# Matrix-LSTM attention before two mixtures of experts: decay by matmuls over gate rows, row-tiled scores, and a new order of attention, routing and experts

## Chip, cores and metric

One core of one Trainium2 chip. The metric is device time in microseconds (us) of one launch; lower is better.

## The reference, cut to what matters

```python
B, H, S, D = 2, 8, 768, 40                       # attention, token by token
m_new  = maximum(f_gate[t] + m, i_gate[t])
f_stab, i_stab = exp(f_gate[t] + m - m_new), exp(i_gate[t] - m_new)
C = f_stab * C + i_stab * outer(v[t], k[t])
n = f_stab * n + i_stab * k[t]
y[t] = sigmoid(o_gate[t]) * (C @ q[t]) / maximum(abs(n @ q[t]), 1)
x = y as (1536, 320)                             # tokens of both batches
noisy = x @ w_gate + log1p(exp(x @ w_noise)) * noise
top2 of 8 experts a token, weights softmax(top2)
out[token] += weight * (relu(x[token] @ w1[e]) @ w2[e])         # F = 1024
out2 = sum over 4 experts of p[:, e] * (relu(out @ v1[e]) @ v2[e])
```

## The kernel before, in words

**Attention.** The 768 tokens of a batch are cut into 6 chunks of 128, so 12 chunks run one behind the other, batch 0 first. The gates stand as 16 rows (batch and head) of 768 columns. `gates` (L234) forms running maxima and decay sums on DVE (VectorE) in four parts (chunk 0, chunk 1, chunks 2 and 3, chunks 4 and 5; each part holds both batches). `gates_turn` transposes the result to token rows, `gates_out` writes the decay sums LF and their exponentials to DRAM. For a chunk, `o_load` brings LF back, copied to all 128 partitions (tile A, 512 KB), and the state's decay gb; `o_decay` makes 8 exponentials of 128x128 on ACT (ScalarE, L333), one per head with that head's bias, and POOL (GpSimd) masks them (L335). `o_S` computes scores: kp holds 4 heads in partitions 0 to 39 and 4 in 64 to 103, zero elsewhere, and each of 8 matmuls contracts 104 rows (L342). `o_M` multiplies scores by A on DVE (L348), `o_AV` and `o_inter` sum values and the state's share (L407, L400), `o_U`, `o_Cu`, `o_Cg` carry the state C, `o_qg` scales queries by gb on POOL (L353), `o_tp` and `o_x` transpose and normalise into x (L428), `o_store` writes x to DRAM. `o_xp` transposes x for the router, `o_lp` and `o_lt` make its logits: three matmuls with the router weights stationary, a copy, a transpose and a reduction.

**The order.** `STEP` (L48) is one step of the pipeline, four pieces; a word such as S1+1 is an operation with the chunk it works on, counted from the step's. 16 steps make 64 pieces. Two strings weave them with other work: in `PLAN1` A is a piece, r a piece of the routing of batch 0, w a split of a weight into two fp32r parts, z and o single loads; `PLAN2` does the same for batch 1 beside the first expert units. The strings set the order in which the program is written and hence the priorities; a scheduler then places each engine's instructions. `route(b, h)` (L473) ranks the 8 logits of half of a batch, counts slots, and scatters token numbers to DRAM with one indirect DMA on POOL per chunk and choice (L540): 8 for the first half, 4 for the second. Then `xload` (L592) gathers an expert's tokens (xe, L598) and `prep` (L605) transposes and splits them.

**Experts.** `UNITS` lists 12 units: experts 0 to 3 on batch 0 (256 columns each), expert 3 on batch 1 (256, unit 4), experts 4 to 7 on both (448), experts 2, 1, 0 on batch 1. A unit is 64 matmuls of stage 1 (L194: 8 blocks of 128 hidden rows, 8 products each) and stage 2 (L208: 3 products per block and token tile). Units 0 to 3 are woven with `PLAN2`; unit 4 is loaded and prepared only after unit 3, when the attention's pools are closed. The second mixture (`moe2`) runs 4 experts over the 1536 tokens in groups of `G2` = 384 columns, 4 groups an expert; `combine` gathers the first mixture's rows into its input.

## Time and profile before

| | us |
|---|---|
| median of 3 runs | 706.52 (706.26, 713.24, 706.52) |
| profiled execution | 711.51, its span 709.5 |
| PE / DVE / ACT / POOL busy in the span | 683.9 / 370.2 / 265.6 / 128.4 |
| mean granted TensorE clock | 0.972 of full speed |

Rows of the profile were read from the one profiled execution. PE is TensorE's matmuls, "PEclk" the granted clock (1.00 is 2.4 GHz, 0.50 is 1.2 GHz). The span has three parts: attention and the first routing up to about 112 us, the 12 expert units up to about 344 us, the second mixture to the end.

### The profile page before, as it was taken

To read this page: it belongs to the slowest core of one execution; us is meant where nothing else is said; L and a number is where in the kernel's file an instruction comes from. 1 tells how busy PE (TensorE), PEld (TensorE's weight loads), DVE (VectorE), ACT (ScalarE), POOL (GpSimd) and SP (SyncE) were. 2 spreads that over 40 slices of the span, in tenths; PEclk is the share of its full clock that TensorE was granted. 3 is DMA by queue.
4 is the path that set the end of the run, shared out by engine and by line. 5 is a ranking of instruction groups with operands and counts; after the bars stand their busy time and mean duration, and the time that the engine had idled before them with its cause. 6 is when DMAs were issued, how large, how long until landed. Compare 5 with 4: busy or idle time off the path is not lost.

```text
span 709.5 us, 11969 instructions
## 1 busy us (share of the span) xinstructions
PE 683.9 (96%) x4683; PEld 656.0 (92%) x4683; DVE 370.2 (52%) x819; ACT 265.6 (37%) x533; POOL 128.4 (18%) x183
## 2 busy tenths in 40 slices
PE   8997888999899999999999999999999999999997
PEld 6776668999799999999999999999999999999997
DVE  7767778885466565658855325332252322423321
ACT  5557546752353444445532214221132212312210
POOL 5453782054501101124042000000000000000000
PEclk7897699999999999999999999999999999999999
DMA  6789657765556454467651004100041000000000
GB/s 186 218 247 283 189 167 237 219 190 146 149 185 192 123 150 139 141 198 232 198 181 52 1 1 120 45 1 1 1 130 34 1 1 16 23 1 29 28 29 31
DMA packets 39948, 80.07 MB, mean 113 GB/s; under 512 B 9376, under 2 KB 16464, under 8 KB 39888
## 3 DMA queue, kind: packets, MB, share of 16 engines
q1 hardware_dynamic: 36496, 70.39, 33.1%
q0 software_dynamic: 3392, 8.86, 4.4%
q8 instruction: 39, 0.64, 0.4%
q14 instruction: 21, 0.17, 0.1%
HBM read 70.20 MB, written 9.04 MB: 112 GB/s over the span
## 4 chain that ended last, share of the span: by engine, by line
PE 89%; DMA 4%; DVE 4%; issue 2%; POOL 0%; ACT 0%; another core or an unknown queue 0%; SPq 0%; ACTq 0%; DVEq 0%
PE z L194 25%; PE z L208 24%; PE s L194 15%; PE s L208 12%; PE sp L342 3%; PE hp L407 2%; PE s L204 1%; PE lp L449 1%; DMA raw<-w 1%; DMA kp<-kT 1%; PE lb L324 1%; PE pa L612 1%; PE hp L400 1%; PE tp L415 1%; DMA gb<-gd 1%
## 5 line engine op out<-in xcount | busy, mean ns | idle before, releaser
L211 ACT ACTIVATE hh<-z 128x384 fp32r<-128x384 f32 x128 | 62.4, 492 | 220.4 <-PE z L194 219.3
L194 PE MATMUL z<-x2h,w1hi 128*128 128x384 f32 x384 | 128.6, 335 | 0.0
L208 PE MATMUL z<-w2lo,hh 128*128 128x320 f32 x384 | 118.8, 309 | 0.5 <-issue 0.3
L208 PE MATMUL z<-w2hi,hh 128*128 128x320 f32 x384 | 119.0, 310 | 0.0
L208 PE MATMUL z<-w2hi,hl 128*128 128x320 f32 x384 | 118.7, 309 | 0.0
L212 DVE SCALAR_TENSOR_TENSOR hl<-z,hh 128x384 fp32r<-128x384 f32 x128 | 69.9, 555 | 84.2 <-ACT hh L211 84.1
L208 PE MATMUL s<-w2hi,hh 128*128 128x320 f32 x448 | 107.8, 313 | 1.2 <-DVE hh L212 1.1
L194 PE MATMUL z<-x2h,w1lo 128*128 128x384 f32 x384 | 107.8, 334 | 0.0
L194 PE MATMUL z<-x2l,w1hi 128*128 128x384 f32 x256 | 85.6, 334 | 0.0
L194 PE MATMUL s<-xh,w1hi 128*128 128x256 f32 (+1 forms) x288 | 84.6, 312 | 0.6 <-issue 0.6
L208 PEld LDWEIGHTS s<-w2hi,hh 128*128 128x128 f32 x448 | 76.8, 188 | 2.7 <-DVE hh L212 1.7
L175 DVE TENSOR_TENSOR w1lo<-raw,w1hi 128x768 fp32r<-128x768 f32 x60 | 57.3, 957 | 38.7 <-ACT w1hi L174 38.0
L175 DVE TENSOR_TENSOR w2lo<-raw,w2hi 128x640 fp32r<-128x640 f32 x60 | 49.2, 822 | 52.5 <-ACT w2hi L174 48.7
L208 PEld LDWEIGHTS z<-w2hi,hl 128*128 128x128 f32 x384 | 72.2, 188 | 0.5 <-issue 0.5
L208 PEld LDWEIGHTS z<-w2lo,hh 128*128 128x128 f32 x384 | 72.2, 188 | 0.4 <-issue 0.4
L208 PEld LDWEIGHTS z<-w2hi,hh 128*128 128x128 f32 x384 | 72.2, 188 | 0.0
L194 PEld LDWEIGHTS z<-x2h,w1hi 128*128 128x128 f32 x384 | 72.1, 188 | 0.0
L194 PE MATMUL s<-xh,w1lo 128*128 128x256 f32 (+1 forms) x288 | 70.6, 309 | 1.2 <-issue 1.2
L194 PEld LDWEIGHTS z<-x2h,w1lo 128*128 128x128 f32 x384 | 70.3, 188 | 0.0
L208 PE MATMUL s<-w2lo,hh 128*128 128x320 f32 x224 | 69.1, 309 | 0.0
L174 ACT CAST w2hi<-raw 128x640 fp32r<-128x640 f32 x60 | 43.4, 728 | 64.5 <-PE s L204 22.9
L174 ACT CAST w1hi<-raw 128x768 fp32r<-128x768 f32 x60 | 49.9, 836 | 45.0 <-PE s L194 18.3
(188 smaller groups left out, 1036.2 us busy)
## 6 DMA issues: line engine op xcount, KB each, us to landing
raw<-w SPq DMA_DIRECT2D x44, 384.0 KB
raw<-w SPq DMA_DIRECT2D x44, 320.0 KB
raw<-v SPq DMA_DIRECT2D x16, 384.0 KB
A<-LFd SPq DMA_DIRECT2D x10, 512.0 KB
raw<-v SPq DMA_DIRECT2D x16, 320.0 KB
kv<-kv SPq DMA_DIRECT2D x12, 324.0 KB
Yd<-ys SPq DMA_DIRECT2D x8, 320.0 KB
qt<-qT SPq DMA_DIRECT2D x12, 208.0 KB
```

The source lines that it names most:

```text
L174: nc.scalar.copy(hi, raw)
L175: nc.vector.tensor_sub(lo, raw, hi.bitcast(F32))
L194: nc.tensor.matmul(out_ps, l, r, start=(i == 0), stop=(i == len(seq) - 1))
L204: nc.tensor.matmul(yp, both[f], r[:, k], start=(f == 0 and i == 0), stop=(f == NF - 1 and i == 1))
L208: nc.tensor.matmul(yp, l, r, start=(f == 0 and i == 0), stop=(f == NF - 1 and i == 2))
L211: nc.scalar.activation(hh, src, AF.Relu)
L212: nc.vector.scalar_tensor_tensor(hl, src, 0.0, hh.bitcast(F32), ALU.max, ALU.subtract)
L324: nc.tensor.matmul(lp[:, j, :], rowsel[:, 4 * g + j, :], LF[:, i, :], start=True, stop=True)
L342: nc.tensor.matmul(sp[:, j, :], t["kp"][:, 4 * g + j, :], t["qt"][:, j, :], start=True, stop=True)
L400: nc.tensor.matmul(hp[:, p, :], Cs[c % 2][:, p, :], t["qg"][:, p, :], start=(p == 0), stop=False)
L407: nc.tensor.matmul(hp[64 * j : 64 * j + 41, p, :], t["kv"][:, 4 * j + p, D:], t["A"][:, 4 * j + p, :], start=False, stop=(p == 3))
L415: nc.tensor.transpose(tp[:, p, :], st[i]["hs"][:, p, :], ident[:105, :105])
```

## The change

Gate rows stand on all 128 partitions (8 copies of the 16, loaded as 768 KB), and `gates_terms` turns them into two operands tk and tq, so that a single matmul per 4 heads gives all the exponents of A in PSUM and a single exponential makes A (`o_decay`). gb comes by a matmul and an exponential too (`o_gb`). The loads of A and gb, and the transposes for the bias, are gone. The products tq and tk are 128x512 each; those of chunk 0 run on DVE, those of chunks 1 to 5 on POOL. Scores are 8 matmuls of 40 rows, alternating between two row groups and two PSUM banks; k comes in one load of 208 KB. The router's logits are 3 matmuls with x stationary and a copy. The scatters are letters s of the plans, one or two beside a piece; the second half's routing (q), the end of the routing (F), gathers (X) and the first `prep` (P) have letters as well. The first expert begins with 12 pieces left. The gathers and `prep` of unit 4 move into unit 3. `G2` is 512, and the first group's stage 1 runs ahead of `combine(1)`.

```diff
-G2 = 3 * P
+G2 = 4 * P
-LEAD = 6
-PLAN1 = "AAAAAAAAAAAzAAoAAAArrwArAwArrrrrArArrrrwrAAArrrArrArAwrrArArAArrrrArrrArA"
+PLAN1 = "Az A Al Al Ag Al Aw A Aw A Aw A Aw A A A Ar Ar Ar Ar Ar Ar Ass Asr Asq Asq Asq Asq Asq Aq Ass AssF Aq AX A AF AF A AP"
...
-    "U+0 D1+2 kw+1 M1+0 loadk+2 S0+1 lp-2 store-3",
-    "qg+1 tp-1 x-1 Cu-1 Cg+0 load+3 inter+0 M0+0 D0+3 lt-2",
-    "",
-    "S1+1 xp-1 AV+0",
+    "U+0 D0+2 D1+2 kw+1 M1+0 loadk+2 lg-2 store-2",
+    "tp-1 x-1 qg+1 M0+0 inter+0 load+3 Cg+0",
+    "G+2",
+    "xp-1 S+1 AV+0 Cu+0",
...
+    def gates_terms(part):
+        n = PARTS[part]
+        nc.scalar.copy(LFh[:, n], LF[:, n])
+        nc.scalar.copy(ash[:, n], asr[:, n])
+        nc.vector.tensor_scalar(flat(LF, n), flat(LF, n), low, keys, ALU.mult, ALU.add)
+        nc.vector.scalar_tensor_tensor(flat(LF, n), flat(LFh, n).bitcast(F32), qsel, flat(LF, n), ALU.mult, ALU.add)
...
+        eng = nc.vector if part == 0 else nc.gpsimd
+        for c in range(n.start, n.stop):
+            wide = lambda x: x.unsqueeze(1).to_broadcast([P, 4, P])
+            eng.tensor_mul(tq[:, c], wide(LF[:, c]), head.unsqueeze(2).to_broadcast([P, 4, P]))
+            last = eng.tensor_mul(tk[:, c], wide(asr[:, c]), quarter.unsqueeze(2).to_broadcast([P, 4, P]))
...
     def sigmoid(b):
+        nc.scalar.preload_act_table_set("sigmoid_and_others")
         nc.scalar.activation(xs[b], xs[b], AF.Sigmoid)
+        nc.scalar.preload_act_table_set("natural_log_exp_and_others")
...
-        for h in range(4 * g, 4 * g + 4):
-            src = t["lb", g][:, h - 4 * g, :] if ("lb", g) in t else A[:, h, :]
-            last = nc.scalar.activation(A[:, h, :], src, AF.Exp, bias=as_t[:, c, b * H + h : b * H + h + 1])
...
+        dp = psum([P, 4, P], "dp")
+        nc.tensor.matmul(dp, tk[:, c, 2 * b + g], tq[:, c], start=True, stop=True)
+        nc.scalar.activation(A, dp, AF.Exp)
...
-    def o_S(i, g):
+    def o_S(i):
         t = st[i]
-        sp = psum([P, 4, P], "sp")
+        sp = [psum([P, 4, P], "sp") for _ in range(2)]
         for j in range(4):
-            nc.tensor.matmul(sp[:, j, :], t["kp"][:, 4 * g + j, :], t["qt"][:, j, :], start=True, stop=True)
...
+            for g in range(2):
+                r = slice(64 * g, 64 * g + D)
+                nc.tensor.matmul(sp[g][:, j, :], t["kp"][r, j, :], t["qt"][r, j, :], start=True, stop=True)
...
-    for w in PLAN1:
...
-    xload(0)
-    xload(1)
-    drain_n(A, LEAD)
-    prep(0)
...
+    drain(follow(PLAN1, 0, 0))
+    RST = follow(PLAN2, 1, ALONE)
...
+    mj_cm = tc.tile_pool(name="m1j", bufs=2, side="right")
+    joint.append(mj_cm.__enter__())
+    xload(ALONE)
+    if ALONE not in preps:
+        prep(ALONE)
+    drain(moe1(ALONE))
...
+                if g == 0:
+                    next(c1)
+                    drain_n(unit, NF // 2)
```

What the new order makes of the engines' queues shows at three places. First PE (matmuls) in one step of the attention, from the state update up to the scores. Before:

```order
L376 MATMUL up_501<-kv,kw 40x41 x8
L342 MATMUL sp_520<-qt,kp_164 128x128 x4
L449 MATMUL lp_525<-xt,wgn 32x128 x3
L415 MATMUL tp_533<-ident,hs 128x105 x4
L400 MATMUL hp_559<-qg,C_188 105x128 x4
L460 MATMUL lt_571<-ident,ls 128x96
L342 MATMUL sp_574<-qt,kp_164 128x128 x4
L438 MATMUL xp_579<-ident,x_85 128x128 x2
L439 MATMUL xp_579<-ident,x_85 64x128
L407 MATMUL hp_559<-A,kv 41x128 x8
```

After, the same step (dp is the exponent of A, gp that of gb):

```order
L388 MATMUL up_604<-kv,kw 40x41 x8
L333 MATMUL dp_614<-tq,tk 128x512
L333 MATMUL dp_618<-tq,tk 128x512
L462 MATMUL lp_627<-wgn,xt_202 128x16 x3
L427 MATMUL tp_633<-ident,hs 128x105 x4
L412 MATMUL hp_649<-qg,C_199 105x128 x4
L342 MATMUL gp_666<-tq,over_91 104x512
L419 MATMUL hp_649<-A,kv 41x128 x8
L450 MATMUL xp_670<-ident,x_103 128x128 x2
L451 MATMUL xp_670<-ident,x_103 64x128
L354 MATMUL sp_676<-qt,kp 128x128
L354 MATMUL sp_677<-qt,kp 128x128
```

The two blocks of four scores have become one run that alternates between two banks (six more rows like the last two follow), three matmuls of 512 columns are new, and the transpose lt is gone.

Second POOL, from batch 0's first scatter (Td) to the experts' first gather (xe). Before:

```order
L540 DMA Td<-toki,slot_89 10240x1 x8
L335 AFFINE_SELECT A<-A 128x512
L368 TENSOR_TENSOR C_190<-C_188,gb 40x4x41 x2
L335 AFFINE_SELECT A<-A 128x512
L353 TENSOR_TENSOR qg<-qt,gb 104x512
L368 TENSOR_TENSOR C_188<-C_190,gb 40x4x41 x2
L335 AFFINE_SELECT A<-A 128x512
L540 DMA Td<-toki,slot_89 10240x1 x2
L335 AFFINE_SELECT A<-A 128x512
L540 DMA Td<-toki,slot_89 10240x1 x2
L353 TENSOR_TENSOR qg<-qt,gb 104x512
L368 TENSOR_TENSOR C_190<-C_188,gb 40x4x41 x2
```

After, up to the last scatter:

```order
L549 DMA Td<-toki,slot_107 10240x1 x2
L335 AFFINE_SELECT A<-A 128x512 x2
L549 DMA Td<-toki,slot_107 10240x1 x5
L365 TENSOR_TENSOR qg<-qt,gb 104x512
L380 TENSOR_TENSOR C_199<-C_197,gb 40x4x41 x2
L549 DMA Td<-toki,slot_107 10240x1
L335 AFFINE_SELECT A<-A 128x512 x2
L380 TENSOR_TENSOR C_197<-C_199,gb 40x4x41 x2
L365 TENSOR_TENSOR qg<-qt,gb 104x512
L549 DMA Td<-toki,slot_107 10240x1 x4
L335 AFFINE_SELECT A<-A 128x512 x2
L380 TENSOR_TENSOR C_199<-C_197,gb 40x4x41 x2
```

The lump of 8 scatters is cut into 2, 5 and 1 with the attention's masks and products between; before, two masks and a qg follow up to the gather, after, one qg. Between first scatter and first gather the list is the same: 12 scatters, 6 masks, 3 qg, 6 C.

Third PE where unit 4's tokens (pa, pb) are transposed. Before, behind the last stage-2 matmul of unit 3 and ahead of unit 4's first:

```order
L208 MATMUL s_141_2374<-w2hi,hh 128x320
L612 MATMUL pa_2441<-ident,xe 128x128 x2
L613 MATMUL pb_2442<-ident,xe 64x128
L612 MATMUL pa_2441<-ident,xe 128x128 x2
L613 MATMUL pb_2442<-ident,xe 64x128
L194 MATMUL s_144_2471<-xh,w1hi 128x256
```

After, between stage 1 and stage 2 of unit 3:

```order
L214 MATMUL s_157_2286<-xh,w1lo 128x256
L624 MATMUL pa_2311<-ident,xe 128x128 x2
L625 MATMUL pb_2312<-ident,xe 64x128
L624 MATMUL pa_2311<-ident,xe 128x128 x2
L625 MATMUL pb_2312<-ident,xe 64x128
L228 MATMUL s_160_2325<-w2hi,hh 128x320
```

The transposes now have the 48 stage-2 matmuls of unit 3 between them and unit 4. Behind the first expert's first matmul, the attention still has to issue on PE: before, xp, a rest of AV, lp, lt, tp, xp, lp, lt; after, tp, the state's share, xp, AV, lp, tp, xp, lp.

## Rows read from the trace of the kernel before

**Rows 1.** Page, part 1: engine, busy us (share of the span), instructions.

```profile
PE 683.9 (96%) x4683; PEld 656.0 (92%) x4683; DVE 370.2 (52%) x819; ACT 265.6 (37%) x533; POOL 128.4 (18%) x183
```

**Rows 2.** Chain that ended last: start us, us, what.

```profile
52.30 7.55 DMA kp<-kT
...
176.90 3.33 DMA xe<-Xall,tok
...
197.61 12.82 PE s L194 x64
...
401.48 11.10 PE z L194 x64
...
694.25 10.58 PE z L208 x72
```

**Rows 3.** Windows: stretch, length, each engine's busy us (instructions), clock, DMA share, GB/s.

```profile
core 0: us, PE busy (x) PEld busy (x) DVE busy (x) ACT busy (x) POOL busy (x), PEclk, DMA share, GB/s
27.80:111.20 83.40, 70.20 (x678) 56.55 (x676) 62.12 (x196) 48.26 (x124) 48.37 (x59) 0.86 0.76 223
41.80:47.70 5.90, 5.90 (x72) 5.00 (x71) 3.90 (x13) 3.45 (x12) 3.43 (x5) 1.00 0.88 272
53.70:65.70 12.00, 8.44 (x73) 6.80 (x73) 9.20 (x32) 9.24 (x18) 3.41 (x5) 0.72 0.98 269
65.70:75.40 9.70, 8.10 (x74) 6.29 (x73) 8.89 (x25) 7.18 (x20) 6.75 (x7) 0.82 0.95 277
75.40:88.00 12.60, 11.03 (x72) 8.36 (x73) 8.67 (x39) 5.92 (x13) 9.04 (x12) 0.52 0.57 166
...
112.40:130.60 18.20, 18.20 (x142) 16.87 (x141) 15.97 (x39) 13.35 (x24) 3.49 (x3) 1.00 0.77 229
...
161.70:176.50 14.80, 14.80 (x115) 14.76 (x114) 8.36 (x25) 4.24 (x8) 6.65 (x7) 1.00 0.54 160
...
176.50:180.60 4.10, 2.23 (x16) 1.46 (x15) 1.92 (x4) 0.85 (x2) 2.90 (x4) 1.00 0.72 213
...
180.60:197.40 16.80, 15.65 (x118) 15.19 (x119) 7.60 (x11) 6.40 (x12) 7.59 (x8) 1.00 0.48 142
```

**Rows 4.** POOL's timeline at scatters and gathers, and PE's first prep: start us, us.

```profile
70.46 1.21 POOL L540 DMA_INDIRECT Td<-toki,slot  x1 [1.56 <-DVE xt L442]
...
101.80 1.01 POOL L598 DMA_INDIRECT xe<-Xall,tok  x1 [0.15 <-issue]
...
109.77 0.38 PE L612 MATMUL pa<-ident,xe 128*128 128x128 f32 x2
```

**Rows 5.** Groups by form: line, engine, operation, count, busy us, mean ns.

```profile
L540 POOL DMA_INDIRECT Td<-toki,slot x24 | 26.9, 1119 | 35.0 <-DVE tmp L545 26.4 <-issue 5.7 <-DVE xt L442 1.6
L335 POOL TENSOR_SCALAR_AFFINE_SELECT A<-A 128x512 f32<-128x512 f32 x24 | 16.7, 701 | 30.9 <-ACT A L333 27.4 <-issue 2.6 <-DMA kv<-kv 0.5
L353 POOL TENSOR_TENSOR qg<-qt,gb 104x512 f32<-104x512 f32 x10 | 13.6, 1358 | 0.0
L368 POOL TENSOR_TENSOR C<-C,gb 40x164 f32<-40x164 f32 x16 | 8.5, 533 | 6.7 <-PE lt L460 1.7 <-DVE sl L527 1.7 <-DVE C L387 1.6
...
L348 DVE TENSOR_TENSOR A<-sp,A 128x512 f32<-128x512 f32 x20 | 13.8, 688 | 5.3 <-DMA qt<-qT 1.5 <-POOL A L335 1.5 <-issue 0.9
...
L272 ACT ACT_TABLE_LOAD x2 | 2.6, 1283 | 0.8 <-PEq L1039 0.8
```

**Rows 6.** PE's timeline in one step, at full clock: values, then half the scores.

```profile
49.37 1.07 PE L407 MATMUL hp<-A,kv 128*41 128x128 f32 x16
50.37 1.16 PE L342 MATMUL sp<-qt,kp 104*128 104x128 f32 x8
```

**Rows 7.** DVE's normalisation beside POOL's product, and the same one later, alone: timelines.

```profile
27.93 2.31 DVE L428 TENSOR_TENSOR x<-xo,rd 128x320 f32<-128x320 f32 x1
...
28.64 1.25 POOL L353 TENSOR_TENSOR qg<-qt,gb 104x512 f32<-104x512 f32 x1
...
65.75 0.48 DVE L428 TENSOR_TENSOR x<-xo,rd 128x320 f32<-128x320 f32 x1
```

More of the change, by code (lines that the diff above doesn't have):

```diff
@@ L548, in route, with scatter, routed_ @@
         yield
-        if h == 0:
-            return
+    scats = []
+    def scatter():
+        b, k, c = scats.pop(0)
+        s = nc.gpsimd.indirect_dma_start(out=Td, out_offset=bass.IndirectOffsetOnAxis(ap=slot[b][:, k, c : c + 1], axis=0), in_=toki[:, b * NC + c : b * NC + c + 1], in_offset=None)
+        for q in rt[b]["prev"]:
+            tc.declare_no_dep(s.ins, q.ins, reason="distinct rows")
+        rt[b]["prev"].append(s)
+    def routed_(b):
+        assert not scats
+        nl, selb, sel = (rt[b][n] for n in ("nl", "selb", "sel"))
+        routed.add(b)
         nc.sync.dma_start(tok[b].rearrange("p e j -> p (e j)"), Td[: P * E1 * NCOL].rearrange("(p j) o -> p (j o)", p=P))
@@ L589, in xload @@
     def xload(n):
[L590 removed]
+        if n >= len(UNITS) or n in xes or n in preps or not routed.issuperset(UNITS[n][1]) or (n > ALONE and not joint):
             return
@@ L906, in body @@
     m1 = m1_cm.__enter__()
-    nc.sync.dma_start(noise, d["noise"])
     def init():
         nc.sync.dma_start(Td[: P * E1 * NCOL].rearrange("(p j) o -> p (j o)", p=P), zidx)
-    def routes(b):
-        for h in range(2):
-            yield from route(b, h)
-        routed.add(b)
     def splits():
@@ L921, in splits, with follow @@
             yield
-    R0 = routes(0)
-    W0 = splits()
-    for w in PLAN1:
-        if w in "zo":
-            init() if w == "z" else og_load(1)
-        else:
-            next({"A": A, "r": R0, "w": W0}[w], None)
-    drain(W0)
-    drain(R0)
-    xload(0)
-    xload(1)
-    drain_n(A, LEAD)
-    prep(0)
-    def rest():
-        R1 = routes(1)
-        for w in PLAN2:
-            if w == " ":
-                yield
-            else:
-                next({"A": A, "r": R1}[w], None)
-        drain(A)
-        drain(R1)
-    RST = rest()
+    def follow(plan, b, first):
+        r, q, f, w = route(b, 0), route(b, 1), routed_(b), splits()
+        for group in plan.split():
+            for t in group:
+                if t in "Arqfw":
+                    next({"A": A, "r": r, "q": q, "w": w}[t], None)
+                elif t == "F":
+                    next(f, None)
+                elif t == "X":
+                    xload(first)
+                    xload(first + 1)
+                else:
+                    {"s": scatter, "l": w_load, "P": lambda: prep(first), "z": init, "g": lambda: sigmoid(1)}[t]()
+            yield
+        for g in (A, r, q, f):
+            assert next(g, None) is None or g is A
+    drain(follow(PLAN1, 0, 0))
+    RST = follow(PLAN2, 1, ALONE)
     for n in range(ALONE):
@@ L970, in body @@
     x2l = x2p.tile([P, 2, B * S], F32R, name="x2l")
-    for n in range(ALONE, LAST0 + 1):
+    for n in range(ALONE + 1, LAST0 + 1):
         drain(moe1(n))
```

264 lines of the change are left out of this document (111 added, 153 removed).

## Prediction, made before the changed kernel was run

> **What bounds the kernel now.** I read the page's busy times first: PE is busy 96% of the span [rows 1], so a gain must take work from PE or close the few holes in it. The chain of waits shows where these are. From 401 us on it alternates between 64 stage-1 and 72 stage-2 matmuls without a gap, up to 704.8 [rows 2]: that part is PE alone. The holes lie ahead of the experts, and at one unit border, where PE waits for gathered tokens [rows 2]. The windows measure the first part [rows 3]: from 27.8 to 111.2 us, ten steps of the attention, PE is busy for 70.2 of 83.4 us, at a granted clock of 0.86, and DVE for 62.1. One step takes 5.90 us when nothing disturbs it, and is then all PE; but 53.7 to 65.7 takes 12.0 (DMA share 0.98, and the chain waits 7.55 us for kp [rows 2]), 65.7 to 75.4 takes 9.7 with DVE busy for 8.89 of them, and 75.4 to 88.0 takes 12.6, at a clock of 0.52, beside the lump of eight scatters on POOL. What counts is when the first expert runs densely: 112.4 us in this trace. Behind that, all is a sum of PE work.
>
> The sum below is made against the profiled execution's 711.5 us, 5.0 above the median of 706.5. The 5.0 are subtracted at the end.
>
> **The change, part by part.**
>
> *Second mixture, 512 instead of 384 columns.* A stage-1 matmul of 384 columns takes 11.10/64 = 173.4 ns, one of 448 12.82/64 = 200.3 [rows 2]: 0.42 ns a column, so 227 ns for 512 and 14.53 us for 64. 16 groups of 11.10 are 177.6, 12 of 14.53 are 174.3: **-3.3**. Stage 2 has the same matmuls. The combination of batch 1 must now be done during the first group; its gathers lie beside 14.5 us of stage 1. If they came late, a gather's wait like 3.33 us [rows 2] would take all of this back.
>
> *Unit 4.* Between unit 3 and unit 4, 4.10 us pass with PE busy for 2.23, some of that thinly [rows 3]. The transposes, about 1 us, stay; moved behind stage 1 of unit 3 they have the 48 stage-2 matmuls ahead of unit 4 as cover for the splits on ACT and DVE: -3.1. Unit 4 itself took 16.80 us, unit 3 14.80 and without a hole [rows 3]; I take back 1.5 of the 2.0, since the gathers of unit 5 still come after the pools close. Together **-4.6**, bounds 0 (the gather is late in its new place too) and -6.1 (the whole 4.10 and the whole 2.0).
>
> *What is left of the attention behind the first expert's start.* Before, the stretch 112.4 to 130.6 took 18.2 against 14.8 of unit 3 [rows 3]: 3.4 us of attention. After, PE still issues tp, the state's share, xp, AV, lp and again tp, xp, lp. An undisturbed step of 5.90 [rows 3] without its scores (twice 1.16 [rows 6]) is 3.6; tp, xp and lp a second time add about half of that, 1.9: 5.5. **+2.1**, bounds 0 (they fall into holes) and +4.
>
> *The start of the experts.* Two sums, for DVE and for POOL, since both wait and are waited for.
>
> DVE: the first normalisation starts at 27.9 [rows 7]. It will come later. For chunk 0, DVE makes tq and tk (two 128x512 products of 0.69 [rows 5] = 1.4) and four passes of 128 columns (below 0.69 each; I take 0.3 = 1.2), and the sigmoid now stands behind them with an exponential table to be reloaded, 1.28 [rows 5]: +3.9, so 31.8. Bounds: nothing if they run in the shade of the first loads (28), or 8 us if all of the larger gate load and POOL's products of chunk 1 come ahead too (36). From there DVE has about the work of before, 62.1: the reductions of the logits go, some splits of expert weights come earlier. What goes are the waits: the loads of A (512 KB a chunk) and gb, the 8 small exponentials per chunk, the lump on POOL. Before, DVE was busy for 62.1/83.4 = 74% of the stretch, in the worst of its own steps for 8.89/9.70 = 92% [rows 3]. Between them, at 83%, 62.1 takes 74.8, and the first dense matmul comes 1.2 later as before: 31.8 + 74.8 + 1.2 = 107.8. Ends: 92% and 28 give 97, 74% and 36 give 121.
>
> POOL: between first scatter and first gather the list is unchanged: 12 scatters, 6 masks, 3 qg, 6 C. With 1.27 a scatter (its 1.12 and the issue between) and the groups' means [rows 5] that is 15.2 + 4.2 + 4.1 + 3.2 = 26.7 of the 31.3 us that it took (70.46 to 101.80 [rows 4]). First scatter after: before it came 42.5 us behind the first normalisation, with 6.1 of these lost in the step of 12.0; it now stands three pieces later, three quarters of a step, 4.9 at 6.5 a step: 31.8 + 42.5 - 6.1 + 4.9 = 73.1. The list then takes between 26.7 and 31.3, 29.0. Before, first gather to dense matmuls took 112.4 - 101.8 = 10.6 [rows 4]; five pieces now lie between, and attention no longer stands between prep and the dense stretch: 9.4. In sum 111.5.
>
> I take the middle, 109.6: **-2.8** against 112.4. The scores' part in it is small: 16 PE instructions took twice 1.16, and 41-column values in pairs 1.07 [rows 6], so paired scores save about 1 us a chunk, while three matmuls of 512 columns (0.68) come in; PE gains some 0.5 us a step, where it is the bound at all.
>
> A trace row speaks against the products on POOL: a normalisation on DVE took 2.31 us while POOL made its mask and qg, and 0.48 with POOL idle [rows 7]. The Trainium skill says this as a rule (SBUF — State Buffer, section "SBUF: two separate sides"): DVE and GpSimd share a port pair under an exclusive lock, so that the loser blocks for the whole instruction, and the trace agrees with its 2.31 against 0.48. Ten products of 1.36 on POOL [rows 5] are 13.6 us in which DVE's two-operand work would stand; this is the slower rival below.
>
> **Sum:** -3.3 - 4.6 + 2.1 - 2.8 = -8.6; 711.5 - 8.6 = 702.9, less 5.0: **698** us. Its own range, with the start between 106 and 112, is 694 to 700.
>
> **Rivals.**
>
> *No earlier start.* POOL's list stays at 31.3 and the later prologue eats the rest: dense at 115. Then 2.6 - 5.8 = -3.2, 703. For it: POOL's list is unchanged, and DVE's busy step is at 92%. Against: the loads that held the step of 12.0 are gone.
>
> *POOL's products hold DVE (slower).* The ten products fall beside the gates and the first steps; if each stops DVE for its 1.36, the start moves by 13.6 to 123.2, and by some 2 more because the prologue is then at its late end: 125, so 12.6 - 5.8 = +6.8, 713. It decides from a start at 118 on (no gain), and from 125 on the loss is over 1%. For it [rows 7]; against: most products are due steps ahead of their use, and DVE has 21 us of idle time in the stretch.
>
> *The undisturbed pace.* If the prologue is no longer than before (28) and the steps take 5.90 throughout, the first scatter, 6.3 steps on, comes at 65; POOL's list in 26.7 and 6.5 behind its first gather (five pieces at that pace) give dense matmuls at about 98. Then -14.4 - 5.8 = -20.2, 686. Against: the routing steps had 8.89 of DVE work each.
>
> *The scores don't pair.* If the two row groups don't overlap, PE keeps 2.3 us for them and the 0.68 is extra: on some eight steps at most 5 us, 703. For it: half the scores took 1.16 although all rows but 40 held zeros. The Trainium skill (TensorE: Matmul & The Clock Gate, section "LDWEIGHTS (loading the stationary operand)") says that a weight load costs by its columns and not its rows; by it the loads of 128 columns, as many as before, gain nothing from 40 rows. The trace can't separate that, since its paired values have 41 columns.
>
> **How the numbers follow.** Forecast 0.42, undisturbed pace 0.14, no earlier start 0.22, unpaired scores 0.05, POOL holding DVE 0.17. A difference of 1% (7.1 us, 699.5 and 713.6) is about what a measurement tells from none. Of the forecast's 0.42, 0.36 lie below 699.5, with the 0.14 that is 0.50 faster; 0.06 + 0.22 + 0.05 and 0.02 of POOL's case make 0.35 the same; 0.15 slower. The range reaches from the undisturbed pace, 686, to 712, close under the slower rival; less than 0.2 is left out.
>
> **What would show it.** The stage-1 pieces of the second mixture at 14.5 us, 12 of them; no hole ahead of unit 4; 18 to 21 us for the first unit; no loads of A in the DMA queues and the DMA share below 0.98 in every step; first normalisation at about 32, first scatter at 73, first gather at 102, dense experts at 110. The forecast is wrong if the dense stretch starts after 114 or before 104; the slower rival shows as normalisations above 1 us beside POOL's tq and tk.

## The result, and the profile after

The changed kernel takes 715.66 us (median of 15 runs, 711.12 to 722.83), beside it on the same chip the kernel before takes 707.13 (15 runs, 704.88 to 713.38). The ratio is 1.0104 with a 95% interval of 1.0079 to 1.0129: slower by 1%, where 698 us and faster had been forecast. Ratios leave out runs that fell into a slower state; medians and ranges hold all runs. The changed kernel's profiled execution took 717.2 us (before 711.5), a difference of 5.7.

The page's first parts after, for [rows 1]: the instructions by engine, and (last line) PE's clock in 40 slices.

```profile
span 715.1 us, 11253 instructions
PE 675.1 (94%) x4411; PEld 617.3 (86%) x4411; DVE 375.5 (53%) x801; ACT 258.1 (36%) x448; POOL 139.0 (19%) x195
...
PEclk7788979999999999999999999999999999999999
```

PE has 8.8 us less to do than before and the span is 5.6 longer: it waits more. The chain of waits shows which parts run as worked out (start us, us, what):

```profile
41.03 1.01 POOL tk L277
42.08 1.10 PE dp L333 x2
...
50.92 6.26 DMA raw<-w
...
80.22 1.09 PE sp L354 x16
...
167.03 3.76 DMA Td<-toki,slot
171.25 3.12 DMA raw<-w
...
177.72 5.33 DMA raw<-w
...
365.01 14.53 PE z L214 x64
...
410.24 14.08 PE z L228 x96
```

A stage-1 piece of 512 columns takes the 14.53 us that the sum had; the scores of one chunk are 16 PE instructions in 1.09 us, where half of them took 1.16 [rows 6]. New in the chain are POOL's tk ahead of dp, and a weight load (raw) at 50.9. The weight loads at 171.3 and 177.7 stand where the chain of before had two as well, of 5.2 us at 155.8 and 2.5 at 170.5. The windows after, for [rows 3] (length, busy us of each engine with instructions, clock, DMA share, GB/s), cut at the normalisations; the first line is the whole stretch from the first normalisation to the experts:

```profile
34.50:117.60 83.10, 68.39 (x680) 55.76 (x679) 63.58 (x189) 37.65 (x78) 50.91 (x61) 0.82 0.53 148
...
34.50:47.00 12.50, 9.41 (x82) 7.91 (x81) 10.15 (x18) 6.26 (x15) 10.40 (x13) 0.81 0.50 160
47.00:54.30 7.30, 7.30 (x83) 6.01 (x84) 7.26 (x15) 4.58 (x9) 4.61 (x6) 0.86 0.72 215
54.30:63.00 8.70, 7.02 (x65) 5.78 (x61) 6.05 (x14) 4.57 (x9) 3.19 (x4) 0.79 1.02 296
...
86.40:98.70 12.30, 6.16 (x78) 5.06 (x78) 6.62 (x26) 3.82 (x9) 9.81 (x13) 0.92 0.42 104
98.70:107.80 9.10, 8.01 (x57) 7.16 (x57) 7.95 (x34) 1.84 (x5) 6.72 (x9) 0.50 0.14 42
118.80:138.10 19.30, 19.30 (x162) 18.80 (x163) 15.82 (x45) 11.25 (x21) 3.46 (x4) 1.00 0.53 157
168.00:192.10 24.10, 20.16 (x137) 19.34 (x137) 9.13 (x18) 5.50 (x10) 9.70 (x10) 0.93 0.53 170
```

The difference of the two traces by place, in us:

| place | before | after | moved | forecast |
|---|---|---|---|---|
| first normalisation | 27.9 | 34.5 | +6.6 | +3.9 |
| from there to dense experts | 84.5 | 84.3 | -0.2 | -6.7 |
| units 0 to 2, from dense | 49.4 | 51.5 | +2.1 | +2.1 |
| units 3 and 4 with their border | 35.6 | 37.9 | +2.3 | -4.6 |
| rest of the units | | | -1.0 | 0 |
| second mixture | 349.5 | 345.3 | -4.2 | -3.3 |

These add to +5.6. So two things went wrong: the start of the experts, and the border of unit 4.

**The start.** In the step from 86.4 to 98.7 PE is busy for half the time. POOL's timeline there, for [rows 4] (start, us, what, in brackets idle before and what ended it):

```profile
84.40 1.20 POOL L549 DMA_INDIRECT Td<-toki,slot  x1 [3.42 <-DVE tmp L540]
...
88.35 0.97 POOL L549 DMA_INDIRECT Td<-toki,slot  x1 [0.16 <-issue]
...
93.42 0.95 POOL L549 DMA_INDIRECT Td<-toki,slot  x1 [0.30 <-DMA Td<-toki,slot]
94.39 1.27 POOL L365 TENSOR_TENSOR qg<-qt,gb 104x512 f32<-104x512 f32 x1
95.61 0.47 POOL L380 TENSOR_TENSOR C<-C,gb 40x164 f32<-40x164 f32 x1
96.78 0.47 POOL L380 TENSOR_TENSOR C<-C,gb 40x164 f32<-40x164 f32 x1 [0.69 <-DMA Td<-toki,slot]
...
113.10 1.00 POOL L610 DMA_INDIRECT xe<-Xall,tok  x1 [0.86 <-issue]
```

Five scatters, 88.35 to 94.4, stand ahead of the small product C on POOL's queue. DVE's next instruction needs that C, and the normalisation stands behind it; DVE's timeline:

```profile
91.19 0.16 DVE L519 TENSOR_TENSOR g<-pp,off 128x16 f32<-128x16 f32 x1
96.12 0.32 DVE L401 TENSOR_TENSOR C<-up,C 40x164 f32<-40x164 f32 x1 [4.76 <-POOL C L380]
...
98.73 0.92 DVE L440 TENSOR_TENSOR x<-xo,rd 128x320 f32<-128x320 f32 x1
```

And PE waits for the normalisation; its timeline, with the first expert matmul below:

```profile
99.79 0.66 PE L450 MATMUL xp<-ident,x 128*128 128x128 f32 x2 [6.64 <-DVE x L440]
...
118.78 0.39 PE L214 MATMUL s<-xh,w1hi 128*128 128x256 f32 x1
```

DVE stands 4.8 us, PE 6.6, and the step behind that (98.7 to 107.8) runs wholly at a clock of 0.50, the lower of the two levels.

**Unit 4.** Its border has no hole any more, and it takes 16.2 us from its first matmul to that of unit 5 where it took 18.7. But unit 3, 16.9 before, takes 21.7. SP's queue there:

```profile
165.05 0.39 SPq L580 DMA_DIRECT2D Wall<-wdense  x1
170.81 0.33 SPq L558 DMA_DIRECT2D tok<-Td  x1
171.25 6.80 SPq L180 DMA_DIRECT2D raw<-w  x5
```

The load of tok (L558) reads the list that the scatters write, so it stands from 165.4 until the last of them has landed (167.03 + 3.76 = 170.8 in the chain): 5.4 us. Five weight loads are queued behind it. ACT's timeline shows their users:

```profile
174.40 0.83 ACT L194 CAST w1hi<-raw 128x768 fp32r<-128x768 f32 x1 [8.56 <-DMA raw<-w]
...
183.08 0.72 ACT L194 CAST w2hi<-raw 128x640 fp32r<-128x640 f32 x1 [6.09 <-DMA raw<-w]
183.71 1.56 ACT L231 ACTIVATE hh<-s 128x512 fp32r<-128x512 f32 x3
```

The hidden values hh stand behind the split on ACT, and PE stands idle from 180.9 to 184.4 for them, in the middle of unit 3. Before, SP waited for that list too (3.5 us, behind the store that ends at 166.6), but with eight weight loads issued ahead of it, from 150.0 on, and one directly behind:

```profile
150.00 14.07 SPq L160 DMA_DIRECT2D raw<-w  x7
...
170.08 0.33 SPq L551 DMA_DIRECT2D tok<-Td  x1
```

### The profile page after: what moved, and what is told of

The parts are those of the page before. It is cut to its first block, busy times and chain, and to the rows that moved or that the text cites. A ratio compares the mean times of both kernels' runs of the same rounds, so it can differ in the third digit from the quotient of the medians.

```text
span 715.1 us, 11253 instructions
## 1 busy us (share of the span) xinstructions
PE 675.1 (94%) x4411; PEld 617.3 (86%) x4411; DVE 375.5 (53%) x801; ACT 258.1 (36%) x448; POOL 139.0 (19%) x195
## 4 chain that ended last, share of the span: by engine, by line
PE 82%; DVE 5%; DMA 5%; POOL 3%; ACT 2%; issue 2%; SPq 0%; POOLq 0%; DVEq 0%; ACTq 0%
PE z L214 24%; PE z L228 24%; PE s L214 13%; PE s L228 12%; DMA raw<-w 2%; DMA Td<-toki,slot 1%; PE s L224 1%; PE sp L354 1%; POOL Td L549 1%; PE lp L462 1%; PE hp L419 1%; PE pa L624 1%; DVE w1lo L195 1%; DVE w2lo L195 1%; DMA fi<-fi 1%
## 5 line engine op out<-in xcount | busy, mean ns | idle before, releaser
L231 ACT ACTIVATE hh<-z 128x512 fp32r<-128x512 f32 x96 | 57.0, 598 | 192.9 <-PE z L214 192.7
L228 PE MATMUL z<-w2lo,hh 128*128 128x320 f32 x384 | 118.5, 309 | 0.0
L214 PE MATMUL z<-x2h,w1hi 128*128 128x512 f32 x288 | 112.5, 391 | 0.0
L232 DVE SCALAR_TENSOR_TENSOR hl<-z,hh 128x512 fp32r<-128x512 f32 x96 | 65.8, 690 | 82.5 <-ACT hh L231 82.5
L214 PE MATMUL z<-x2h,w1lo 128*128 128x512 f32 x288 | 96.7, 390 | 0.0
L195 DVE TENSOR_TENSOR w2lo<-raw,w2hi 128x640 fp32r<-128x640 f32 x60 | 50.4, 842 | 66.3 <-ACT w2hi L194 66.2
L195 DVE TENSOR_TENSOR w1lo<-raw,w1hi 128x768 fp32r<-128x768 f32 x60 | 59.2, 987 | 34.7 <-ACT w1hi L194 34.2
L194 ACT CAST w2hi<-raw 128x640 fp32r<-128x640 f32 x60 | 43.5, 728 | 87.7 <-PE s L224 25.2
L214 PE MATMUL z<-x2l,w1hi 128*128 128x512 f32 x192 | 74.9, 390 | 0.0
L214 PEld LDWEIGHTS z<-x2h,w1lo 128*128 128x128 f32 x288 | 54.1, 188 | 11.3
L214 PEld LDWEIGHTS z<-x2h,w1hi 128*128 128x128 f32 x288 | 54.1, 188 | 10.8
```

The costliest lines, as they stand in the source:

```text
L194: nc.scalar.copy(hi, raw)
L195: nc.vector.tensor_sub(lo, raw, hi.bitcast(F32))
L214: nc.tensor.matmul(out_ps, l, r, start=(i == 0), stop=(i == len(seq) - 1))
L228: nc.tensor.matmul(yp, l, r, start=(f == 0 and i == 0), stop=(f == NF - 1 and i == 2))
L231: nc.scalar.activation(hh, src, AF.Relu)
L232: nc.vector.scalar_tensor_tensor(hl, src, 0.0, hh.bitcast(F32), ALU.max, ALU.subtract)
```

## The experiments

Each ratio is against the kernel before on the same chip, whose medians on the chips used were 707.1 to 713.7. "Start" is the first expert matmul (before 111.3, after 118.8). Where an expectation says "fifth", chunk 5 counted from 0 is meant (normalised at 65.8 before, at 78.6 after).

A ratio also holds what happens behind the start. In the changed kernel's profiled execution, and in its versions in the second, third and fourth set, unit 1 took 16.6 to 17.0 us. In all its versions in the first and the last set (e1, e2, e3; s4, s5, s7), which ran on two other chips, it took 18.7 to 22.0, whatever the edit; why is open.

**First set: prologue, products, tok, and 512 alone.** Theory T: the prologue's order and POOL's products delay the start. Rivals: clock, routing.

e1, the gates of later chunks held back behind the first terms:

```diff
-    gates_terms(0)
-    gates(1)
+    last = gates_terms(0)
+    with tc.issue_after(last):
+        last = gates(1)
```

(the same for gates(2), and gates(3) behind chunk 0's state update.)

> The changed kernel, with the gate scans of chunk 1 held behind chunk 0's tq and tk on DVE, and those of chunks 2 and 3 behind chunk 1's. Theory (the prologue's order on DVE sets when the attention starts): chunk 0's decay scan, at 12.2 us in the changed kernel behind all the scans of the later chunks, comes near 7; the first normalisation moves from 34.5 to about 29, the dense experts from 122 to about 117, the time falls by 4 to 6 us. Rival (POOL's products and the pace of the later steps bind, so the prologue's slack is eaten): the first normalisation moves, the experts' start moves by less than 2 us, the time by less than 2.

Measured: ratio 1.026 [1.019, 1.033], start 117.8, first normalisation at 39.8, later and not earlier. PE's timeline shows a new wait ahead of it:

```profile
28.01 0.47 PE L284 MATMUL pt<-ident,awr 128*128 128x128 f32 x1 [2.55 <-ACT w_t L285]
...
33.06 1.22 PE L333 MATMUL dp<-tq,tk 128*128 128x512 f32 x2 [4.58 <-POOL tk L277]
```

The chunk-0 scan came earlier (12.2 to 5.5), but the late gates pushed POOL's tk for chunk 2 back (from 27.4 to 31.7), and that chunk's dp stands ahead of chunk 0's tp on PE. So holding the order delays the first normalisation. The start came 1.0 earlier all the same; the longer time lies behind it, in units 0 and 1 (42.2 us, 36.0 in the changed kernel).

e2, all products on DVE:

```diff
-            eng = nc.vector if part == 0 else nc.gpsimd
+            eng = nc.vector
```

> The changed kernel, with the ten products tq and tk of chunks 1 to 5 on DVE instead of POOL. Theory (POOL, busy for 22.6 of 26 us between 21 and 47, holds the first two steps): the products cost DVE 10 x 0.68 = 6.8, POOL is freed of 12 us, the step from the first to the second normalisation falls from 12.5 to about 8, the time by 3 to 5 us. Rival (DVE is the bound there, busy for 22.2 of the same 26 us): the products are added to its list, the time is the same or up to 5 us longer.

Measured: 1.021 [1.014, 1.029], first normalisation at 41.4, start 118.5. The first normalisation comes 6.9 us later than in the changed kernel and the start where it was: what happens that early does not set the start.

e3, the load of tok on POOL's queue:

```diff
-        nc.sync.dma_start(tok[b].rearrange(...), ...)
+        nc.gpsimd.dma_start(tok[b].rearrange(...), ...)
```

> The changed kernel, with the loads of the token lists (tok) issued on POOL's queue instead of SP's. Theory (in unit 3 SP stands 5.4 us at the load of tok, which waits for the last scatter, with five weight loads behind it; PE idles 4 us for these weights): the stretch from unit 3's start to unit 4's first matmul falls from 24 to about 20, the time by 3 to 4 us. Rival (the weight loads wait for raw buffers that DVE frees, and SP's stand is only the last of the waits): less than 1 us.

Measured: 1.014 [1.009, 1.019]; unit 3 19.1 instead of 21.7, so SP's queue is the cause of its hole. The whole gains nothing: units 0 and 1 took 44.3 us (36.0 in the changed kernel). The start (120.0) and the 65.3 us at the half clock ahead of it are those of the changed kernel run once more (c1 below: 119.7 and 64.9).

e4, the kernel before with `G2` 512 and its loop:

```diff
-G2 = 3 * P
+G2 = 4 * P
```

> The kernel before, with the second mixture in groups of 512 columns and the first group's stage 1 ahead of the combination, as the change has it, and nothing else. Theory (the second mixture is PE alone): 4 us faster than before, 703; the trace of the changed kernel has 345.5 us for it against 349.7. Rival (part of the gain is given back by late gathers of the combination): 1 to 2 us faster.

Measured: 0.9989 [0.9960, 1.0018]. The second mixture took 345.3 us as in the changed kernel (349.5 before), yet the whole can't be told from no change, though 4.2 us less would be a ratio of 0.994. In the trace unit 3 (19.1 against 16.9) and the last unit (19.4 against 16.5, up to the second mixture) give it back; why they are longer isn't accounted for.

**Second set: leave the terms out, and scores alone.** c1 is the changed kernel again, with no edit, as a control.

> The changed kernel as it is, beside the others of this set on the same chip, with a trace of its own. Both theories: 1.01 of the kernel before; the second normalisation near 47, dense experts near 120, a hole in PE of 4 us inside unit 3.

Measured: 1.0059 [1.0020, 1.0099], with start 119.7, PE idle 93.2 to 100.1 and 181.5 to 185.0: both holes recur. Its window from the first normalisation to the experts:

```profile
34.80:118.50 83.70, 72.01 (x679) 59.78 (x678) 63.96 (x189) 38.14 (x77) 50.28 (x60) 0.74 0.51 144
```

With no edit the mean clock there goes from 0.82 to 0.74, the time at the half clock ahead of the start from 51.2 to 64.9 us, the start by 0.9, and one normalisation takes 1.55 us instead of 0.76. Differences of this size between two traces show nothing of an edit.

p1 makes the terms of chunk 0 alone:

```diff
         n = PARTS[part]
+        if part > 0:
+            return None
...
-        nc.tensor.matmul(dp, tk[:, c, 2 * b + g], tq[:, c], start=True, stop=True)
+        nc.tensor.matmul(dp, tk[:, 0, 2 * b + g], tq[:, 0], start=True, stop=True)
...
-            nc.tensor.matmul(gp, over[b], tq[:, c], start=True, stop=True)
+            nc.tensor.matmul(gp, over[b], tq[:, 0], start=True, stop=True)
```

> The changed kernel without the decay terms of chunks 1 to 5: gates_terms returns at once for them, and all chunks use chunk 0's tq and tk (so the decay and with it the output are not the reference's). That takes 8 passes on DVE in each of three parts and the ten products on POOL away. Theory (the terms and products of the prologue are the loss): the second normalisation moves from 47 to about 38, the dense experts from 120 to about 111, the time falls by 8 to 10 us against the changed kernel. Rival (the later steps' pace and the routing set the experts' start): the second normalisation moves, the start of the experts by less than 4 us.

Measured: 1.011 [1.001, 1.021]. First normalisation at 30.2 (34.5), last scatter 106.5 (107.7), start 117.9 (118.8). Taking ten POOL products and the passes of DVE away makes the prologue 4.3 us shorter and the start 0.9 earlier (1.9 against c1), and the time is no less than c1's on the same chip (717.8 against 714.5): the theory that they delay the start falls.

h1, the kernel before with row-tiled scores, the short logits and 512:

```diff
-    "U+0 D1+2 kw+1 M1+0 loadk+2 S0+1 lp-2 store-3",
+    "U+0 D1+2 kw+1 M1+0 loadk+2 lg-2 store-3",
...
-    "S1+1 xp-1 AV+0",
+    "S+1 xp-1 AV+0",
...
-G2 = 3 * P
+G2 = 4 * P
```

(lt-2 goes with lp-2; o_S, the rows of q and k and the logits are those of the change.)

> The kernel before with three parts of the change that don't touch the gates: row-tiled scores with one load of k, logits by three matmuls with x stationary, groups of 512 in the second mixture. Theory (what these parts save on PE is real, and the gate rows alone cost): 1 us less PE work a chunk, dense experts 3 to 5 us earlier than before, 4 us less in the second mixture: 699 to 702 where before has 707. Rival (the start is bound by DVE and POOL, so PE's saving there is worth nothing): only the second mixture's 4 us or less.

Measured: 0.9996 [0.9947, 1.0045], start 113.0 instead of 111.3. Its windows from first normalisation to experts:

```profile
26.20:113.00 86.80, 74.57 (x685) 63.19 (x684) 56.58 (x187) 47.23 (x120) 46.68 (x57) 0.68 0.75 216
```

The clock is 0.68 where before has 0.86 [rows 3]. Busy time times clock, 50.7 against 60.4, is a rough estimate of PE's work in it: about 10 us less work, spent at a lower clock, in a stretch 3.4 us longer.

**Third set: clock and early weights.** w1 warms PE with 32 matmuls ahead of the first work instead of 11:

```diff
-WARM = 11
+WARM = 32
```

> The changed kernel with 32 instead of 11 warm-up matmuls on zeros at the start, so that PE works on until about 14 us instead of idling from 5.6 to 13.8. Theory (PE's idle stretches cost twice, since its granted clock is 0.50 behind them and the steps are PE work): the half-clock stretch of 7 to 24 us shrinks, the work from 14 us on goes faster, the second normalisation comes 2 to 4 us earlier and the experts 1 to 3. Rival (DVE and POOL bind the prologue, PE's clock there is free): the clock may rise, the normalisations and the experts stay within 1 us.

Measured: 1.0105 [1.0068, 1.0142], the ratio of the changed kernel, start 117.0. The edit didn't do what it was for: from 14 to 24 us the clock was 0.50 as without it, and from 35 to 50 it was 0.50 where the changed kernel had 0.77. So what the prologue's clock costs isn't shown.

v1 issues the first expert's loads behind chunk 3's store (and PLAN1 has their letters l and w later):

```diff
-        nc.sync.dma_start(raw, d[f"{src}{k}"][e, q])
+        if pos[0] < 4:
+            with tc.issue_after(st[3]["store"]):
+                nc.sync.dma_start(raw, d[f"{src}{k}"][e, q])
+        else:
+            nc.sync.dma_start(raw, d[f"{src}{k}"][e, q])
```

> The changed kernel with the first expert's weight loads held behind the store of chunk 3's x (and their letters l and w eight to ten pieces later), so that their transfers and their splits on ACT and DVE leave the steps before. Theory (the early weights hold the attention: ACT waits 3.1 us for raw at 55 us with the exponentials queued behind it, DMA share 1.02 there): the steps from the second to the fifth normalisation take 6.0 to 6.6 instead of 7.3, 8.7, 7.7; the first scatter comes 3 to 5 us earlier, the experts 2 to 4. Rival (the work is only moved: the splits fall into the routing steps, which are PE at a low clock and DVE): earlier normalisations, but the experts' start within 1.5 us.

Measured: 1.0124 [1.0078, 1.0169]. The normalisations of chunks 0 to 5 come at 35.0, 45.9, 51.9, 57.8, 63.3 and 74.8: three steps of 5.4 to 6.0 us, at last the undisturbed pace of before, instead of 7.3 to 8.7. Then the held work comes: start 120.7. The early loads and splits do slow the early steps, and held back they slow the late ones.

v3 joins w1, v1 and e3.

> The changed kernel with three edits together: 32 warm-up matmuls, the first expert's weights held behind the store of chunk 3, and the token lists loaded on POOL's queue. Theory (each takes a wait away that stands in another part): 5 to 9 us under the changed kernel, about the kernel before or 1% under it; unit 3 without its hole of 4 us. Rival (only the hole in unit 3 counts): 2 to 4 us under the changed kernel.

Measured: 1.017 [1.014, 1.021], unit 3 16.2, start 127.3. Unit 3's hole is gone, and the start is worse.

**Fourth set: POOL's queue.** The theory formed then: the start hangs on the products that stand behind scatters on POOL. s1 takes C's product from POOL to DVE:

```diff
-                nc.gpsimd.tensor_mul(Cs[1 - c % 2][r, :, e], ...)
+                nc.vector.tensor_mul(Cs[1 - c % 2][r, :, e], ...)
```

> The changed kernel with the state's products C (o_Cg) on DVE instead of POOL, nothing else. Theory (the scatters on POOL hold C, C holds DVE and PE, and the routing behind them): PE's hole of 6.6 us near 93 to 100 us shrinks below 2, the last scatter of batch 0 comes 4 to 6 us earlier, the first expert matmul at 112 to 115 instead of 119; the time falls by 4 to 7 us. Rival (the start follows the fifth normalisation at 78 us, with some 29 us of routing behind it, whatever is in between): the hole closes, the last scatter stays at 106 to 108 and the time within 2 us.

Measured: 1.0078 [1.0041, 1.0115], start 115.7, last scatter 103.4. PE's hole of 6.6 has become 4.16 and ends on DVE:

```profile
97.86 2.01 PE L412 MATMUL hp<-qg,C 104*105 104x128 f32 x8 [4.16 <-DVE slot L535]
```

DVE and POOL in that hole:

```profile
93.32 2.57 DVE L567 TENSOR_TENSOR mx<-lk 128x6 f32<-128x6 f32 x1
...
94.60 1.26 POOL L365 TENSOR_TENSOR qg<-qt,gb 104x512 f32<-104x512 f32 x1
```

An operation on 128x6 that takes 0.17 us in the changed kernel lasts until POOL's masks and qg beside it have ended (95.86). So more than half of the hole is DVE's work standing beside POOL's other product, and not behind it in a queue.

s2 takes qg to DVE as well, and batch 1's tok to POOL's queue:

```diff
-            nc.gpsimd.tensor_mul(qg, st[i]["qt"], st[i]["gb"])
+            nc.vector.tensor_mul(qg, st[i]["qt"], st[i]["gb"])
...
-        nc.sync.dma_start(tok[b].rearrange(...), ...)
+        (nc.gpsimd if b else nc.sync).dma_start(tok[b].rearrange(...), ...)
```

> As s1, with the product qg on DVE too and the token list of batch 1 loaded on POOL's queue. Theory: the gain of s1, and 3 to 5 us from unit 3, which falls from 21.7 to about 17: 8 to 11 us under the changed kernel, 704 to 707. Rival: only the part of unit 3.

Measured: 705.78 us, ratio 0.9946 [0.9913, 0.9978] in ten runs (703.6 to 709.0). The changed kernel was not run beside it; its medians elsewhere are 714.5 and 715.7, 9 to 10 us more. Start 110.2, last scatter 98.4, unit 3 16.6. Its windows, the first from the first normalisation to the experts, the last unit 3:

```profile
35.40:109.00 73.60, 61.50 (x674) 49.96 (x671) 61.47 (x210) 36.92 (x76) 30.59 (x36) 0.89 0.55 159
...
80.90:87.70 6.80, 6.80 (x89) 5.76 (x90) 5.92 (x23) 3.63 (x8) 5.28 (x6) 0.96 0.52 128
87.70:95.10 7.40, 6.58 (x83) 5.17 (x79) 7.24 (x33) 3.33 (x8) 5.60 (x8) 1.00 0.42 105
95.10:100.70 5.60, 4.97 (x69) 4.37 (x69) 5.46 (x24) 0.83 (x4) 3.30 (x4) 1.00 0.11 33
...
164.20:180.80 16.60, 15.69 (x119) 15.30 (x119) 7.68 (x13) 5.10 (x10) 10.20 (x11) 1.00 0.71 217
```

The routing steps take 5.6 to 7.4 us, at a clock of 0.96 to 1.00, beside the same scatters.

b2 is the kernel before with C on DVE, tok of batch 1 on POOL's queue, and 512.

> The kernel before with C on DVE, the token list of batch 1 on POOL's queue, and groups of 512 columns in the second mixture. Theory (the same wait stands in the kernel before: PE idles at 73.8 to 76.1 and 96 to 98 beside its scatters): first expert matmul 2 to 4 us earlier, 4 us from the second mixture: 699 to 702 where before has 707. Rival: only the second mixture, at most 4 us.

Measured: 0.988 [0.982, 0.994], six runs spread from 699.1 to 711.8 with median 706.49 beside s2's 705.78 (by the medians of all runs its ratio would be 0.995); start 111.2, as before. So s2 is the best of the versions on the new order, and the old order with two of its edits does no worse.

p2 joins p1 and v1:

> The changed kernel without the decay terms of chunks 1 to 5 (all chunks use chunk 0's tq and tk, so that decay and output are not the reference's) and with the first expert's weights held behind the store of chunk 3. Theory 2 (several small causes delay the fifth normalisation, and the experts follow it by 40 us): fifth normalisation, at 78.6 in the changed kernel, near 66, first expert matmul near 108. Theory 1 (the stall between scatters, C and DVE): fifth normalisation near 66 to 70 as well, but first expert matmul still above 114.

Measured: 1.0115 [1.0078, 1.0151]. Chunk 5's normalisation comes at 68.1, 10.4 earlier than in the changed kernel; the last scatter only 3.1 earlier (104.6), the start 4.0 (114.8). What the early steps gain is mostly lost again between chunk 5's normalisation and the last scatter (36.5 us, 29.1 in the changed kernel). The held weights' splits fall there as well as the stall at POOL's queue; the run doesn't part them.

**Last set: which edit of s2 counts.** s4 is s2 without its tok edit, s5 the changed kernel with that edit alone, b3 the kernel before with row-tiled scores, 512 and all of s2's edits, s7 is s2 with v1.

s4:

> The changed kernel with the products C and qg on DVE instead of POOL, and the token lists on SP's queue as they were. Theory (POOL's scatters held the attention, and that is most of the late start): first expert matmul at 110 to 112, PE without a hole above 2 us between 85 and 100, unit 3 still with its hole (about 21 us); 5 to 7 us under the changed kernel. Rival (the gain of s2 came with unit 3 alone): within 2 us of the changed kernel.

s5:

> The changed kernel with the token list of batch 1 loaded on POOL's queue, nothing else. Theory (SP stands at that load with five weight loads behind it): unit 3 falls from 21.7 to about 17, the start of the experts is unchanged (117 to 120); 3 to 5 us under the changed kernel. Rival (weights are late for another reason, s2 closed the hole by its earlier start): unit 3 stays above 20.

b3:

> The kernel before with all the parts that have gained or cost nothing: row-tiled scores with one load of k, logits by three matmuls, C and qg on DVE, the token list of batch 1 on POOL's queue, groups of 512; the gates, the decay rows from DRAM and the order of the pieces as before. Theory (the gate rows gain nothing): at or under s2, 0.985 to 0.995 of before. Rival (the gate rows pay once POOL is free, since the loads of A hold the steps near 60 us): slower than s2.

s7:

> s2 with the first expert's weights held behind the store of chunk 3. Theory (with POOL's stall gone, earlier normalisations now move the experts too): fifth normalisation at 63 to 66 instead of 71.6, first expert matmul 2 to 4 us earlier than s2's 110.2, the time 1 to 4 us under s2. Rival (the weights' splits then fall into the routing steps): first expert matmul at 110 or later, the time that of s2 or more.

Measured: s4 1.012 [1.008, 1.016], start 119.4; s5 1.0069 [1.0036, 1.0102], start 119.5; b3 0.9994 [0.9962, 1.0026], start 113.4; s7 1.0099 [1.0066, 1.0132], start 121.4. None gains. s4's windows against s2's:

```profile
72.00:81.20 9.20, 9.20 (x63) 7.55 (x58) 6.44 (x31) 5.32 (x10) 2.12 (x3) 0.50 0.35 111
81.20:94.00 12.80, 9.30 (x87) 7.06 (x88) 6.50 (x24) 3.73 (x8) 8.26 (x10) 0.77 0.33 74
94.00:103.50 9.50, 9.50 (x69) 8.06 (x65) 6.68 (x32) 2.22 (x5) 1.85 (x3) 0.50 0.28 75
```

Up to 81 us the two run alike (chunk 6 normalised at 81.2 and 80.9), with the same instructions on POOL and DVE. Then s4's PE has holes at 86.4, 87.9 and 91.6, is at 0.50 in the step behind them, and its next normalisation comes at 94.0 where s2's comes at 87.7. The first hole lies between two transposes of one group, and the profile shows nothing that PE waits for ("issue"):

```profile
87.48 0.43 PE L427 MATMUL tp<-ident,hs 105*128 105x105 f32 x3 [1.10 <-issue]
```

DVE then waits 4.0 us for PE, and neither waits for POOL. So this loss isn't POOL's queue. The tok edit of batch 1 takes effect only long behind this place, and s4 ran on another chip, so what parts the two is not settled; s2 itself ran on one chip only.

In s5 and s7 unit 3 still takes 21.2: SP's wait is gone, but batch 1's routing ends so late that PE waits for the gathers of unit 4 instead. The load of tok begins 3.5 (s5) and 1.8 us (s7) behind unit 3's first matmul; in s2, where unit 3 takes 16.6, it is 0.1, and in v3 0.5 ahead. s7's PE:

```profile
187.80 0.66 PE L628 MATMUL pa<-ident,xe 128*128 128x128 f32 x2 [2.92 <-DMA xe<-Xall,tok]
```

## Why the prediction was wrong

**Second mixture, -3.3: right** in mechanism and nearly in size: -4.2, with pieces of 14.53 us as worked out. Batch 1's combination cost no wait.

**What is left of the attention, +2.1: right**, as 1.1 in unit 0 (19.3 against 18.2 [rows 3]) and 1.0 in units 1 and 2. That it comes out to the tenth is luck: c1 repeats it, but unit 0 took 20.9 to 22.3 in ten of the other thirteen traces on the new order.

**Unit 4, -4.6: it was +2.3.** The step "the transposes stay; moved behind stage 1 of unit 3 they have the 48 stage-2 matmuls as cover" came true, and unit 4 got 2.5 shorter. What failed is that only PE, ACT and DVE were followed. The gathers need tok, so the load of tok moved earlier too, on SP's queue, which the sum never went through: there it waits for the last scatter with five weight loads behind it, and these are what unit 3's second half needs. The cover became the hole. Shown by e3, v3 and s2, where that load has another queue and unit 3 takes 19.1, 16.2 and 16.6. With s5 and s7 the bound that the prediction gave ("the gather is late in its new place too") shows as well, when the routing ends late.

**The start, -2.8: it was +6.4 from dense to dense.** By place, it is +6.6 up to the first normalisation, +6.2 from there to chunk 5's, +0.1 from there to the last scatter (29.1 us against 29.0), and -6.5 behind it. So the stall at POOL's C lies in a stretch that is no longer than before: it takes away what the forecast had hoped for, and the loss against before lies ahead of it. By the steps of the sum:

- First normalisation 31.8: measured 34.5, inside its bounds of 28 to 36. Of these, 4.3 belong to the terms of chunks 1 to 5 (p1: 30.2). This term mattered little: p1 gave back 4.3 at the front, and 0.9 at the start.
- "Between them, at 83%, 62.1 takes 74.8": the step that failed. DVE's busy time was well estimated (63.58 against 62.1), but it took 83.1 us: DVE busy for 77%, barely above the 74% of before. The waits that go were replaced by new ones: the early loads of weights (raw, 6.26 us in the chain, DMA share 1.02 from 54.3 to 63.0) instead of kp and A, and POOL's C behind five scatters. In s2, with both products off POOL, the same stretch took 73.6 us at 61.47/73.6 = 84%, what the step had assumed.
- First scatter 73.1: measured 84.4, of which 2.7 come from the normalisation; the rest is steps of 7.3 to 8.7 us, and one of 12.5, where 6.5 was put. With v1 three of these steps fall to 5.4 to 6.0, so the weights' early work is what made them long; but it then falls on later steps.
- POOL's list in 29.0: measured 28.7 (84.40 to 113.10). First gather to dense in 9.4: measured 5.7. Both better than forecast.

The sum listed POOL's instructions between scatter and gather and found the list the same. It never asked who waits for each. Before, eight scatters stood in one lump with two masks behind them; now they are cut in pieces with C and qg between, and through C they stop DVE (4.8 us), through DVE the normalisation and PE (6.6 us). From chunk 5's normalisation to the last scatter the changed kernel needs 29.1 us, before needed 29.0; w1 and p1, which change the prologue, need 28.8 and 27.6; s1, with C off POOL, 28.0, s2 26.8. That this wait is there is shown (DVE's row at 96.12; in s1, with C on DVE, it is gone). How much of s2's 9 to 10 us is due to it, how much to POOL's products beside DVE's work (below) and how much to PE's clock is not settled, since s4 with the same product edits on another chip didn't gain.

**PE, "some 0.5 us a step, where it is the bound at all".** By busy time times clock, PE's work between first normalisation and experts fell from 60.4 to 68.39 x 0.82 = 56.1, an estimate of 0.4 a step: about right, though c1, the same kernel, gives 72.01 x 0.74 = 53.3. The sums for DVE and POOL had no third one for PE at its granted clock, and that was a gap: from 47.0 to 54.3 PE is busy throughout, at 0.86, in s2 from 71.6 to 80.9 as well, at 0.50. In the changed kernel 51.2 us ahead of the experts run at the lower level (64.9 in c1), 37.5 before. h1 shows the pattern by itself: less work, clock 0.68, no gain.

**The rivals.** *No earlier start*: the start came at 118.8 instead of 115, with the later prologue in it (+6.6) but with POOL's list at 28.7 and not 31.3. *POOL's products hold DVE*, 713: by sign and size the nearest case, but not by its mechanism. Its mark was normalisations above 1 us beside tq and tk. In the profiled execution they run from 476 to 919 ns; the one of 1.55 us in c1 stands beside qg, and p1, without tq and tk of chunks 1 to 5, has one of 1.55 beside qg too. p1 starts 0.9 us earlier, not 13.6. So these ten products don't set the start. But DVE's work does stretch beside POOL's: what DVE's instructions between first normalisation and start take above the usual time of the same instruction adds up to 9.3 us before, 11.3 after, 13.6 in s1 and 2.2 in s2 (an estimate: what exceeds the tenth percentile of the same line and shape in that trace by over 0.1 us), nearly all of it beside POOL's masks and products. s2 takes this away together with the order of POOL's queue, so no run parts the two. *The undisturbed pace* was reached for three steps in v1 and no further. *The scores don't pair*: they do, 68 ns a PE instruction (1.09/16) against 145 ns before (1.16/8 [rows 6]). At 80.2 the 16 instructions start two by two, 10 ns apart at most, each pair after the second some 110 ns behind the last; at 50.4 before they start singly, some 110 ns apart. The Trainium skill (TensorE: Matmul & The Clock Gate, section "LDWEIGHTS (loading the stationary operand)") counts a weight load by its columns and not its rows. The trace agrees: the loads of 40 rows take as long as those of 104, before and after (ns, least, median, most):

```profile
L342 PEld LDWEIGHTS sp<-qt,kp x192: 186/192/338, 9.5 to 103.9; 104*128 104x128 f32 x192
...
L354 PEld LDWEIGHTS sp<-qt,kp x192: 182/188/334, 18.0 to 117.0; 40*128 40x128 f32 x192
```

So the gain is the overlap of the pairs. Whether row groups alone or the two PSUM banks as well are needed for it, no run shows.

The range ended at 712 with the slower case just outside. What it lacked was a rival in which the moved loads and scatters block their own queues; 717 us in the profile is 14 above the sum's 702.9, of which 9.2 lie in the start and 6.9 at unit 4.

## What to carry to other kernels

When work is moved, walk every queue that its DMAs pass, SP's and POOL's included, and ask for each instruction behind a waiting one who waits for it in turn: a list that stays the same in sum can still put a small product behind five scatters, or five weight loads behind a load that waits. A gain in the early steps counts only if the resource that ends last behind them also gets free sooner, so test it by leaving the suspected cost out altogether before mending it. And where PE has holes, count its work at the granted clock that the trace shows, not at full speed. Run the unedited kernel again beside its variants, too: two traces of it here differ by 0.9 us in the start and by 14 us in the time at the half clock.
